# First k of an attention-and-FFN kernel cast and transposed in two parts, the opening in a written order, and batch 0's column blocks partly at full width

## Chip, cores, metric

The kernel runs on one core of one Trainium2 chip. The metric is the device time of one execution in microseconds (us). A profiled execution also has a span, from the first to the last instruction of the program, which is a little shorter than its time.

The engines are named as in the profile: PE is TensorE, which multiplies matrices; PEld is its loading of weights, which runs beside it; DVE is VectorE; ACT is ScalarE; POOL is GpSimd; SP is SyncE. POOL and SP only issue transfers here, but for one small copy of POOL's per batch.

## What is computed

```python
# q, k, v: 8 batches x 12 heads x 448 positions x 64;  w_in: 768 x 2048;  w_out: 2048 x 768
scores = (1 / sqrt(64)) * q @ k.transpose(0, 1, 3, 2)
attn = maximum(scores, 0.0) ** 2 / 448
a = attn @ v                                  # per head 448 x 64
x = a.transpose(0, 2, 1, 3).reshape(3584, 768)
h = x @ w_in
g = 0.5 * h * (1 + erf(h / sqrt(2)))          # exact gelu
out = g @ w_out                               # 3584 x 768, float32
```

There is no softmax: a score goes through a ReLU and a square, so nothing has to be reduced over a row before the product with v.

## The kernel before

**The work of one batch.** The twelve heads make three groups of four (G = 3). For a group, q and k come in with positions on the partitions and are transposed, so that the 64 head dimensions of two heads lie on 128 partitions (qT and kT). A *step* (L523) is one of seven blocks of 64 key positions of a group: four matmuls of 64x64 weights, which stand side by side on PE, against 448 query positions. ACT makes the ReLU with the scale (L535), or DVE does (L537), and DVE squares the result (L544). When all seven steps of a group are squared, 28 matmuls with v (L585) give the group's part of the attention, which DVE (L301) or ACT (L303) copies into xT, already transposed for the FFN. The first FFN matrix works in 16 *column blocks* of 128 (L632): six matmuls over the 768 features each, and a gelu on ACT (L644). The second (L675) works in tiles of 128 tokens over pairs of batches; DVE copies its output, and SP stores it.

**Buffers.** PSUM has three buffers for the attention (tag w: scores and the product with v) and two for everything else (tag f: transposes, column blocks, output tiles). So a set of transposes cannot start until the one before last has been evicted, and a step not until a ReLU has freed its buffer.

**Transposes.** Batches 0 and 1 are transposed by PE with an identity matrix: `add_tk` (L429 in the profile) does the k of a group with 14 small matmuls into one buffer, which one instruction evicts into kT; `add_tq` (L454) does q's. Batches from 2 on are reordered by DVE (pk and pq) and transposed by transfers that SP issues.

**The opening.** The first group's q and k come in float32 over two queues (q32 on SP's, k32 on ACT's), and are cast by `early`: q on ACT, k (896 columns) on DVE. All other loads are issued by POOL and are cast on the way; a program order lists them, and each issue past the eighth waits until the eighth before it has landed. Until data come, PE runs 45 small matmuls on zeros. Batch 0 is worked in two halves of 224 query positions (`halves`): the first half of q for the three groups is loaded and transposed first, and a step of a half is paired with another, so that one ReLU still covers 896 columns. The column blocks of batch 0 are also passed in halves: for each half a pair of blocks (m and m+1) fills one PSUM buffer with 12 matmuls of 224 rows. Batch 1 and later are worked at full width.

**The order.** All work is recorded first as `Op` objects with estimated durations, dependences and the buffers they need. `Scheduler.run` then picks, engine by engine, the operation with the earliest estimated start plus a bias, and at last issues all operations sorted by their estimated start. From batch 2 on the PE order and POOL's order are given as lists (`pe_q`, `pool_q`); for batches 0 and 1 the estimates and biases decide. `order_only` and `later` are conditions for the planner alone: they hold operations back in the plan and put no wait in the program. Engines execute their own instructions in program order.

## Time and profile before

| | |
|---|---|
| median of 6 runs | 393.6 us (392.91 to 394.33) |
| the profiled execution | 392.91 us, of which the span is 391.1 us |
| PE busy | 380.3 us, 97% of the span |
| DVE, ACT busy | 188.3 us (48%), 200.4 us (51%) |
| POOL busy | 45.7 us (12%) |
| granted PE clock | 0.998 of full speed |
| column blocks (L632) | 864 matmuls, 672 with 448 rows and 192 with 224 |
| chain of work that ended last | PE 94%, ACT 2%, DVE 1%, transfers 1% |

The profile page shows an average over the whole span. PE is busy for 97% of it, and what it lacks lies mostly in the first 32 us, so the views that matter are those by stage: busy time of each engine in a window, what an engine waited for, and the instructions in order of time. A matmul's row lasts longer than its place in the pipeline, since its end is modelled; the distance between starts, or the length of a merged run of matmuls, is the better price. The column "idle before" of an instruction tells how long its engine stood still ahead of it and which instruction ended that; "issue" there means that nothing the profile shows was waited for.

### The profile page before, as it was taken

How to read it: one execution, taken by the hardware profiler on the slowest of the kernel's cores; microseconds unless marked ns; L12 is line 12 of the kernel's file. 1: busy time of each engine (PE TensorE's matmuls, PEld its weight loads, DVE VectorE, ACT ScalarE, POOL GpSimd, SP SyncE). 2: the span in 40 equal slices, each digit the busy share in tenths (PEclk: the TensorE clock that was granted, in tenths of full speed). 3: DMA queues.
4: the chain of work that ended last, by engine and by line, in shares of the span. 5: the costliest groups of instructions: out<-in, count | busy, mean ns of one | idle time of the engine just before them, and what ended most of it. 6: DMA issues, size and time to landing. Idle time of an engine off the chain costs nothing.

```text
span 391.1 us, 8085 instructions
## 1 busy us (share of the span) xinstructions
PE 380.3 (97%) x3496; PEld 216.7 (55%) x3497; DVE 188.3 (48%) x348; ACT 200.4 (51%) x304; POOL 45.7 (12%) x69
## 2 busy tenths in 40 slices
PE   6789999999999999999999999999999999999996
PEld 6566784455555555555555555555555555555563
DVE  3989940486636444644555346545355352110121
ACT  3998845754536554565734466366536645222200
POOL 8665304001100200020000200000000000000000
PEclk9999999999999999999999999999999999999999
DMA  9999997999976791689129871370102011100132
GB/s 176 194 203 204 201 195 115 210 200 193 172 136 130 127 178 42 130 145 162 42 65 152 124 136 42 75 148 3 42 21 62 0 42 42 40 15 27 42 80 80
DMA packets 69523, 42.94 MB, mean 110 GB/s; under 512 B 37744, under 2 KB 65904, under 8 KB 69488
## 3 DMA queue, kind: packets, MB, share of 16 engines
q0 software_dynamic: 30512, 22.47, 38.4%
q1 hardware_dynamic: 38672, 19.49, 22.6%
q8 instruction: 27, 0.44, 0.5%
q10 hardware_dynamic: 304, 0.48, 0.3%
q14 instruction: 8, 0.07, 0.0%
HBM read 45.61 MB, written 11.01 MB: 145 GB/s over the span
## 4 chain that ended last, share of the span: by engine, by line
PE 94%; ACT 2%; DVE 1%; DMA 1%; issue 0%
PE psh L632 38%; PE pso L675 38%; PE ps L523 9%; PE pav L585 8%; ACT a_sq L535 2%; DMA k<-in_k_dram 1%; PE tp L429 0%; PE tp L454 0%; DVE xT L301 0%; DVE a_sq L544 0%; DVE a_sq L537 0%; ACT xT L303 0%; ACT qT L303 0%; DVE nk L301 0%; ACT kT L303 0%
## 5 line engine op out<-in xcount | busy, mean ns | idle before, releaser
L632 PE MATMUL psh<-xT,win_sb 128*128 128x448 bf16 (+1 forms) x864 | 154.7, 332 | 0.0
L675 PE MATMUL pso<-wout_sb,h_sb 128*128 128x384 bf16 (+2 forms) x895 | 151.6, 326 | 0.1
L535 ACT ACTIVATE a_sq<-ps 128x896 bf16<-128x896 f32 x142 | 123.9, 916 | 48.2 <-PE ps L523 48.1
L544 DVE TENSOR_TENSOR a_sq<-a_sq 128x896 bf16<-128x896 bf16 (+1 forms) x169 | 100.3, 617 | 53.0 <-ACT a_sq L535 53.0
L644 ACT ACTIVATE h_sb<-psh 128x448 bf16<-128x448 f32 x128 | 70.0, 548 | 99.3 <-PE psh L632 99.0
L675 PEld LDWEIGHTS <-h_sb 128*128 128x128 bf16 x896 | 86.2, 98 | 62.6 <-issue 5.9
L632 PEld LDWEIGHTS <-win_sb 128*128 128x128 bf16 x864 | 81.7, 98 | 65.7 <-issue 9.0
L301 DVE COPY osb<-pso 128x384 f32<-128x384 f32 (+2 forms) x56 | 31.2, 557 | 89.4 <-PE pso L675 89.4
L523 PE MATMUL ps<-qT,kT 64*64 64x448 bf16 (+1 forms) x756 | 47.3, 336 | 3.6 <-ACT a_sq L535 1.3
L537 DVE TENSOR_SCALAR a_sq<-ps 128x896 bf16<-128x896 f32 x27 | 29.4, 1089 | 40.8 <-PE ps L523 40.8
L585 PE MATMUL pav<-a_sq,v_sb 64*64 64x448 bf16 (+1 forms) x756 | 37.1, 330 | 1.6 <-issue 0.9
L523 PEld LDWEIGHTS <-kT 64*64 64x64 bf16 x756 | 18.8, 105 | 24.5 <-issue 17.6
L585 PEld LDWEIGHTS <-v_sb 64*64 64x64 bf16 x756 | 21.2, 107 | 13.9 <-issue 3.8
L301 DVE CAST xT<-pav 128x448 bf16<-128x448 f32 (+1 forms) x29 | 16.0, 558 | 10.6 <-PE pav L585 5.6
L303 ACT CAST xT<-pav 128x448 bf16<-128x448 f32 (+1 forms) x25 | 12.6, 505 | 15.5 <-PE pav L585 9.1
L498 POOL COPY gate<-qT 128x4 bf16<-128x4 bf16 x5 | 0.9, 189 | 158.0 <-DMA qT<-pq 158.0
L250 POOL DMA_DIRECT2D nq<-in_q_dram x14 | 11.6, 830 | 3.5 <-ACT a_sq L535 2.1
L352 POOL DMA_DIRECT2D v_sb<-in_v_dram x14 | 10.6, 759 | 2.4 <-DMA win_sb<-in_moe_w_in_dram 1.7
L334 POOL DMA_DIRECT2D nk<-in_k_dram x13 | 10.0, 769 | 4.7 <-DMA win_sb<-in_moe_w_in_dram 1.1
L390 DVE COPY pq<-nq 112x512 bf16<-112x512 bf16 x36 | 8.2, 283 | 0.0
L379 DVE COPY pk<-nk 128x896 bf16<-128x896 bf16 x18 | 6.2, 384 | 0.0
L775 PE MATMUL spin<-zero 128*128 128x128 bf16 x45 | 4.2, 281 | 1.0 <-DVE zero L762 1.0
(25 smaller groups left out, 42.4 us busy)
## 6 DMA issues: line engine op xcount, KB each, us to landing
nk<-in_k_dram POOLq DMA_DIRECT2D x5, 672.0 KB, 9.1
nq<-in_q_dram POOLq DMA_DIRECT2D x5, 672.0 KB, 11.8
v_sb<-in_v_dram POOLq DMA_DIRECT2D x5, 672.0 KB, 14.2
out_dram<-osb SPq DMA_DIRECT2D x7, 336.0 KB, 2.8
wout_sb<-in_moe_w_out_dram POOLq DMA_DIRECT2D x2, 1152.0 KB, 11.9
out_dram<-osb SPq DMA_DIRECT2D x8, 288.0 KB, 2.9
v_sb<-in_v_dram POOLq DMA_DIRECT2D x9, 224.0 KB, 8.1
out_dram<-osb SPq DMA_DIRECT2D x8, 240.0 KB, 2.8
```

Of the source, the lines that this page charges most:

```text
L250: nc.gpsimd.dma_start(nq[b][:, 4 * g0 : 4 * g1, c0 * D : c1 * D], q_view(b, g0, g1, c0, c1))
L301: V.tensor_copy(dst, src)
L303: A.copy(dst, src)
L352: nc.gpsimd.dma_start(vt[b][:, 2 * g0 : 2 * g1], kv_view(v, b, g0, g1))
L523: nc.tensor.matmul(ps[64 * j : 64 * j + 64, e, x * w : x * w + w], kT[r, g, i * 128 + 64 * j : i * 128 + 64 * j + 64], qT[r, 2 * g + j, co ...
L535: A.activation(ar, ps, AF.Relu, scale=c_att)
L537: V.tensor_scalar(ar, ps, c_att, 0.0, op0=mybir.AluOpType.mult, op1=mybir.AluOpType.max,)
L544: V.tensor_mul(box["a2"][:, :, :used], ar, ar)
L585: nc.tensor.matmul(pav[0][o2 : o2 + 64, e, :w], vt[b][r, 2 * g + e, bass.ts(i, D)], box["a2"][r, e, o : o + w], start=(i == 0), stop=(i == ...
L632: nc.tensor.matmul(ph[:, x * n : x * n + n], win_sb[:, kd, bass.ts(m + x, 128)], xT[b][:, kd, c], start=(kd == 0), stop=(kd == KD - 1),)
L644: A.activation(hT[b // 2][:, m : m + nm, o + c.start : o + c.stop], box[0][:, :S].rearrange("p (x n) -> p x n", x=nm), AF.Gelu,)
L675: nc.tensor.matmul(po[:, :w], hT[pr][:, kf, bass.ts(t, 128)], wout_sb[:, kf, c], start=(kf == 0), stop=(kf == KF - 1),)
```

## The change

There are three parts.

1. The first k is cast in two instructions, 512 columns (blocks 0 to 3) on DVE and 384 (blocks 4 to 6) on ACT, and its transposes are two sets with an eviction each (`K_CUT = 4`). `add_tk` takes a range of blocks, and a step depends only on the set that holds its block.
2. `ORDER` lists all work of the opening, batches 0 and 1 and the loads and reorderings that lie among it. P, A, D, G and S stand for PE, ACT, DVE, POOL and SP; the number is the operation's place in the order in which the kernel records it. The listed operations are issued in the listed order; what is not in the list follows as before. The two planner conditions go. Estimated starting times of engines and landings change too, which are only for the planner.
3. `HALF_M = 6`: only the column blocks 0 to 5 of batch 0 are passed in halves; blocks 6 to 15 are passed one by one with 448 rows, when both halves of batch 0's attention are there.

In the written order, the first operations are: P11, A10 and D12 are the first q's transposes, cast and eviction; D13 and A16 the two casts of k; P14, A15 and P17, D18 the two sets of k's transposes with their evictions; P21 and D22 the q of group 1; P39, P33 and P36 the first steps, with the ReLUs D40, A34 and A37; P19 and P23 are the k transposes of groups 1 and 2. P27, P29 and P31 transpose the second half of q, P129 to P139 batch 1's k and q, and P141 is the first column block.

```diff
-TQ_AFTER = 1
+HALF_M = 6
...
-COLD_END = 4.0
+COLD_END = 0.0
+K_CUT = 4
 SPIN = 45
+ORDER = """
+G0 G1 G2 G3 G4 G5 A10 D13 G6 A16 P11 P14 G7 D12 A15 P17 G8 D18 P21 P39 D22 P33 P36 A34 D40
+P19 D20 A37 P23 G9 P42 P48 D24 P54 A43 D35 A49 P51 D44 P25 D38 A52 D41 G117 A55 D53 P45 D50
+A26 D47 A46 P57 D56 P69 P66 A58 D70 P27 G118 A67 P29 D59 P63 G119 A28 D71 P60 A64 G120 D68
+P78 D61 A62 P75 A79 D65 P81 P31 D30 A76 D80 P96 G121 D32 A97 P72 D77 G122 A82 D98 P129 G123
...
+P205 D230 A209 P261 D182 P251 D183 A262 D210 A206 D233 P202 A252 S237 D207 D232 P226 D234
+A203 D204 S238 S239 P269
+"""
...
-        rest = [o for o in self.open if id(o) not in inside]
+        names = {"P": "PE", "A": "ACT", "D": "DVE", "G": "POOL", "S": "SP"}
+        gone = set()
+        for word in ORDER.split():
+            op, eng = self.open[int(word[1:])], names[word[0]]
+            _, dur, lat = next(e for e in op.engines if e[0] == eng)
+            self.commit(max(self.ready(op), self.free[eng]), op, eng, dur, lat)
+            gone.add(id(op))
+        fixed = {e: [o for o in v if id(o) not in gone] for e, v in fixed.items()}
+        rest = [o for o in self.open if id(o) not in inside | gone]
...
-        for est, op, eng in sorted(self.log, key=lambda x: x[0]):
+        n = len(ORDER.split())
+        for est, op, eng in self.log[:n] + sorted(self.log[n:], key=lambda x: x[0]):
             op.fn(eng)
...
-    def add_tk(b, g, bias=T_BIAS, after=()):
-        box = []
+    def add_tk(b, g, i0=0, i1=NK, bias=T_BIAS):
+        box, n = [], 128 * (i1 - i0)
...
-            for i in range(NK):
+            for i in range(i0, i1):
...
-    ld_k[0, 0] = [early("DVE", lambda: nk[0][:, :2], k32, 4.7)]
-    add_tk(0, 0)
+    ld_k[0, 0] = []
+    for eng, i0, i1 in (("DVE", 0, K_CUT), ("ACT", K_CUT, NK)):
+        c = slice(i0 * D, i1 * D)
+        o = early(eng, lambda c=c: nk[0][:, :2, c], k32[:, :, c], 5.45)
+        ld_k[0, 0] += [o] * (i1 - i0)
+        add_tk(0, 0, i0, i1)
...
-        add_tq(0, g, HC, NC, T_LATE, [later(lambda: AV[0, TQ_AFTER, 0].start)])
+        add_tq(0, g, HC, NC, T_LATE)
...
-        half = [order_only(AV[0, G - 1, 0])]
-        add_tk(1, g, T_ONE, half)
-        add_tq(1, g, bias=T_ONE, after=half)
-    for m in range(0, KF, 2):
+        add_tk(1, g, bias=T_ONE)
+        add_tq(1, g, bias=T_ONE)
+    for m in range(0, HALF_M, 2):
         add_f1(0, m, 0, bias=F1_BIAS)
...
-    for m in range(0, KF, 2):
+    for m in range(0, HALF_M, 2):
         add_f1(0, m, 1, bias=F1B_BIAS)
+    for m in range(HALF_M, KF):
+        add_f1(0, m, bias=F1B_BIAS)
```

## The prediction, made before the result was known

> **What bounds the kernel now.** I read the 40 slices first, then busy time by stage, then what TensorE (PE) waited for, then the opening in order of time. The slices show PE full from the fourth on, while VectorE (DVE) and ScalarE (ACT) are full only in the opening:

> ```profile
> PE   6789999999999999999999999999999999999996
> DVE  3989940486636444644555346545355352110121
> ACT  3998845754536554565734466366536645222200
> ```

> Busy time by stage (length, then PE, PEld, DVE, ACT, POOL with instruction counts, granted clock, DMA share, GB/s):

> ```profile
> 6.00:8.20 2.20, 1.40 (x38) 1.00 (x38) 1.43 (x3) 0.00 (x0) 2.20 (x3) 1.00 1.37 202
> 8.20:12.00 3.80, 2.86 (x88) 2.12 (x84) 3.60 (x6) 3.75 (x5) 3.40 (x6) 1.00 1.43 198
> 12.00:20.00 8.00, 6.31 (x184) 4.74 (x177) 7.42 (x17) 7.77 (x14) 5.23 (x8) 1.00 1.48 192
> 20.00:32.00 12.00, 10.09 (x238) 7.31 (x238) 11.02 (x21) 10.16 (x16) 6.87 (x11) 1.00 1.27 204
> 32.00:58.00 26.00, 25.97 (x354) 20.44 (x349) 20.02 (x39) 19.71 (x31) 7.61 (x11) 1.00 1.28 202
> ```

> From 32 us on PE is the bound (25.97 of 26.00), and the changed order listing is the old one again from batch 1's first column block on; so only PE's idle time before 32 us, and PE work itself, can be won. Idle: 0.80 in 6-8.2, 0.94 in 8.2-12, 1.69 in 12-20, 1.91 in 20-32, together 5.34 us. From 8.2 to 20 us the other two engines hold it: DVE 11.02 and ACT 11.52 of 11.8 us. What PE waited for:

> ```profile
> PE ps L523 <- ACT a_sq L535: 1.3, 3, 0.5
> PE pav L585 <- issue: 0.9, 1, 0.9
> PE ps L523 <- ACT qT L303: 0.7, 2, 0.4
> PE ps L523 <- DVE kT L301: 0.7, 1, 0.7
> PE pav L585 <- ACT a_sq L535: 0.6, 2, 0.3
> ```

> The last number is the longest: no wait is large but the one with no releaser ("issue"). The opening:

> ```profile
> 5.35 0.62 ACT L303 CAST nq<-q 112x512 bf16<-112x512 f32 x1 [2.61 <-DMA q<-in_q_dram]
> 5.52 0.89 DVE L301 CAST nk<-k 128x896 bf16<-128x896 f32 x1 [4.50 <-DMA k<-in_k_dram]
> 6.45 0.39 DVE L301 COPY qT<-tp 128x448 bf16<-128x448 bf16 x1
> 7.09 0.62 DVE L301 COPY kT<-tp 128x896 bf16<-128x896 bf16 x1 [0.24 <-PE tp L429]
> 7.77 0.58 PE L523 MATMUL ps<-qT,kT 64*64 64x224 bf16 x16 [0.72 <-DVE kT L301]
> 8.21 0.92 ACT L535 ACTIVATE a_sq<-ps 128x896 bf16<-128x896 f32 x1 [2.24 <-PE ps L523]
> 8.40 1.09 DVE L537 TENSOR_SCALAR a_sq<-ps 128x896 bf16<-128x896 f32 x1 [0.69 <-PE ps L523]
> ```

> ACT stands still from 5.97 to 8.21 behind a serial chain: cast of k, transposes, eviction of kT.

> **1. Ten column blocks at full width.** Batch 0 issued 16x12 matmuls of 224 rows; now 72 of 224 and 60 of 448: 60 pairs become 60 single ones. Prices, from the chain of waits:

> ```profile
> 51.19 16.09 PE psh L632 x120
> 67.28 0.50 PE ps L523 x8
> 116.11 1.13 PE psh L632 x6
> ```

> Six full ones take 1.13, so 189 ns each. The 120 are 72 halves (six pairs of blocks) and 48 full: (16.09 - 48x0.189)/72 = 97 ns. A pair costs 2x97 - 189 = 5 ns too much; 60 of them 0.3 us (0 if halves are exactly half). The mean durations of the two shapes, 260 and 353 ns, contain the pipeline and would say three times too much per instruction.

> **2. Changes of kind on PE.** Two attention steps (8 matmuls of 448, four side by side, 2x0.19) take 0.50 between column blocks, and the block behind them 1.24 instead of 1.13: about 0.2 us per visit. Counted in the two order listings up to the eighth column block of batch 1, PE changes between transposes, attention and FFN 36 times before and 34 times now: one visit, 0.2 us (0 to 0.3, as places differ).

> **3. First k in two parts.** The listing puts the cast of 512 columns on DVE, 384 on ACT behind the cast of q; then q's transposes, 8 of k's, q's eviction (DVE), the first k eviction (ACT), 6 transposes, their eviction (DVE), the q transposes of group 1, and only then the first step. ACT starts its next instruction about 0.12 before the last one's row ends (five ReLUs of 0.92 in 4.17 us: 0.81 apart), DVE 0.08. The shapes are new. 512 float32 columns on DVE lie between 0.38 (448, bf16) and 0.69 (512 to float32, in the tail): 0.57, so 5.52 to 6.09. 384 on ACT lie between the rows of 224 (0.36) and 448 (0.53): 0.48, so 5.85 to 6.33. The first k eviction (512 on ACT, rows 448: 0.53, 896: 0.91, so 0.58) runs 6.6 to 7.2. The second set needs the buffer that q's eviction frees at 6.84; evicted 7.15 to 7.5. Group 1's q needs the buffer freed at 7.2: 7.25, evicted on DVE 7.6 to 8.0. First step at 7.7 (before 7.77), first ReLU on DVE at 8.0 (8.40), on ACT at 8.1 (8.21). So the split gains little in itself: two waits for buffers replace the long chain. What it gives is work in ACT's empty stretch. By now q of group 1 is evicted as well (0.30 of DVE, formerly at 9.41), and kT of group 1 goes to DVE (0.53) instead of ACT (0.79). DVE is ahead by 0.40+0.30-0.53 = 0.17, ACT by 0.1+0.79 = 0.89. Both bound the stretch, so half the sum: 0.5 us; from 0.1 (the first ReLU alone) to 0.9 (ACT alone).

> [...]

> **4. The "issue" wait.** At 26.05 PE stops inside an AV group for 0.92 us, with no semaphore. The page has 27 packets of 0.44 MB on the instruction queue for 3496+3497 PE instructions: 16 KB, about 259 instructions each. The stall comes 256 instructions after 21.0 us. The three stretches of 256 up to it took 6.6, 5.8 and, without the stall, 4.8 us; with it 6.0. I read it as code that needs about 5.8 to 6.0 us to come while the queues are full. In the changed listing the same 256 hold two pairs of column blocks instead of one; 24 such instructions take 1.26 us, 24 of attention about 0.35. So about 4.8+0.9 = 5.7 us: a stall of 0.3 where 1.1 stood. The stretch ahead loses its only pair, but waits more: near 5.4 us, a stall of up to 0.4 that partly lies under ACT. I take a gain of 0.6; bounds -0.3 (both stall in full) and 1.1 (none).

> [...]

> **5. Order in 20-32 us.** Besides the issue wait, 0.99 us is idle there. Part is its aftermath: ACT idles 0.61 at 27.1 and PE then waits for ACT to free buffers. Another part is ACT's idle 1.13 ahead of a half eviction at 30.98, which waits for DVE's half. In the listing two sets of transposes and three steps follow that AV group, and full-width blocks stand between steps of batch 1. I take 0.4, bounds 0 and 1.0. Behind batch 1's last AV only one block (1.13) instead of six pairs now covers the eviction that batch 1's own blocks need (0.62 on DVE); if it slips, up to 0.6 is lost, and I cost it at nothing.

> POOL and SP carry the same instructions in the same order. Removing the planner's conditions has no instruction of its own.

> **Sum.** 0.3+0.2+0.5+0.6+0.4 = 2.0 us. Span 391.1 to 389.1; the profiled execution 392.91 to 390.9; the median shown, 393.6, lies 0.7 above that execution, so 391.6.

> **Rivals.** (a) *The code packets stay as they are.* One stall of 1 us or two of half remain wherever PE runs attention densely. For it: the cause is the full queues, DMA share 1.2 to 1.5 in every opening stage, and the change moves no load. Against it: the longer stretch. Gain 2.0-0.6-0.4 = 1.0, since the aftermath stays: 392.6. (b) *ACT and DVE bound the opening whatever the order.* For it: 98% and 93% busy from 8.2 to 20 us, and nearly the same work for both. Against it: ACT's 2.2 empty us. Terms 1 and 2 alone: 0.5, so 393.1. (c) *Slower: the order runs into the loads.* Issue plus time to landing gives q's second half at 6.61+8.2 = 14.8, k of batch 1 at 12.58+7.3 = 19.9, its q at 15.40+5.8 = 21.2. Before, PE takes these at 16.38, 21.59 and 24.56, at least 1.6 us later. The new order puts them ahead of other steps, right at their landing, with AV and QK queued behind. Landings later by D cost D once; above 2.0 the kernel is slower, and 3.0 gives 393.6-2.0+3.0 = 394.6. For it: the queue is never empty here. Against it: POOL's issues are the same. That the order is not what it says is excluded by the listing.

> **Chances.** Forecast 0.60, (a) 0.20, (b) 0.13, (c) 0.07. A measurement tells about 0.2% (0.8 us) from no change. Forecast and most of (a) (0.17) count as faster, and 0.02 of (b): 0.79; the rest of (a) and (b), 0.14, as no change; (c) 0.07 as slower. The range runs from a gain of 3.0 (terms 3 to 5 near their upper bounds) to (b)'s 0.5: 390.6 to 393.1.

> **What would show it.** Right: L632 (another line number then) with 804 matmuls; two short casts of k; first step at 7.7, ReLUs at 8.0 and 8.1; the issue wait under 0.5; PE idle in 6-32 us down from 5.3 to about 3.8; first step of batch 2 at 65.3 instead of 67.28. Wrong: PE waiting for nq or nk loads at 15-29 us; a second issue wait; a wait for xT ahead of batch 1's blocks.

## The result, and the profile after

The changed kernel takes 392.5 us in the median of 24 runs (391.77 to 394.38), the kernel before 393.85 us in 54 runs on the same chips (392.62 to 395.45). The ratio is 0.9971, with a 95% interval of 0.9963 to 0.9979: a gain of 1.1 us (0.8 to 1.5), where 2.0 was forecast. The profiled execution took 393.52 us with a span of 391.7; it is one of the longest of its kind, for a reason given below. L632 is now L644 and has 804 matmuls.

The slices of the page, of the changed kernel:

```profile
PE   7899999998999999999999999999999999999996
PEclk9899999999999999999999999999999999999999
```

PE is fuller in the opening, but the tenth slice (88 to 98 us) is an 8 where before all were 9, and the clock has an 8 in the second. Busy time by stage of the changed kernel, with the columns as in the prediction (length, PE, PEld, DVE, ACT, POOL with counts, clock, DMA share, GB/s) and one stage more:

```profile
6.00:8.20 2.20, 1.63 (x42) 1.33 (x46) 0.98 (x3) 1.20 (x3) 2.20 (x3) 1.00 1.34 197
8.20:12.00 3.80, 3.05 (x96) 2.25 (x85) 3.56 (x7) 3.28 (x5) 3.21 (x6) 1.00 1.43 198
12.00:20.00 8.00, 6.49 (x144) 4.63 (x137) 6.94 (x14) 6.82 (x11) 4.99 (x8) 0.79 1.48 192
20.00:32.00 12.00, 11.31 (x276) 8.82 (x273) 11.32 (x23) 10.96 (x18) 7.16 (x11) 1.00 1.26 199
82.00:92.00 10.00, 8.68 (x89) 4.60 (x87) 7.13 (x19) 4.89 (x7) 0.00 (x0) 1.00 1.36 193
```

From 20 to 32 us only 0.69 is idle, where 1.91 was. The clock of 0.79 in the third row is the mean of that stage: it fell to half from 16.0 to 19.4 us. The last row has 1.32 idle between 82 and 92 us, where PE stood still for nothing before:

```profile
82.00:92.00 10.00, 10.00 (x100) 5.50 (x99) 8.21 (x20) 5.75 (x8) 0.00 (x0) 1.00 1.23 196
```

The same stages in a second profile of the changed kernel (e1, span 390.7), with a full clock:

```profile
6.00:8.20 2.20, 1.71 (x46) 1.32 (x50) 1.07 (x3) 1.11 (x3) 2.20 (x3) 1.00 1.36 201
8.20:12.00 3.80, 3.51 (x96) 2.33 (x88) 3.79 (x8) 3.52 (x5) 3.40 (x6) 1.00 1.43 198
12.00:20.00 8.00, 5.72 (x164) 3.97 (x163) 7.50 (x15) 7.48 (x13) 5.15 (x8) 1.00 1.48 193
20.00:32.00 12.00, 11.25 (x257) 8.72 (x251) 11.19 (x22) 10.65 (x18) 6.78 (x11) 1.00 1.27 204
82.00:92.00 10.00, 8.93 (x90) 4.58 (x89) 7.99 (x20) 5.47 (x7) 0.00 (x0) 1.00 1.39 182
```

What PE waited for, changed kernel: the "issue" wait of 0.9 is gone, a wait for DVE's ReLU has come, at 91 us, and one for a load of q, at 15 us.

```profile
PE ps L535 <- DVE a_sq L549: 0.9, 1, 0.9
...
PE tp L465 <- DMA nq<-in_q_dram: 0.5, 1, 0.5
```

The opening of the changed kernel in order of time:

```profile
5.40 0.43 DVE L308 CAST nk<-k 128x512 bf16<-128x512 f32 x1 [4.38 <-DMA k<-in_k_dram]
6.10 0.51 ACT L310 CAST nk<-k 128x384 bf16<-128x384 f32 x1
...
7.93 0.77 PE L535 MATMUL ps<-qT,kT 64*64 64x224 bf16 x24
...
8.37 1.09 DVE L549 TENSOR_SCALAR a_sq<-ps 128x896 bf16<-128x896 f32 x1
8.56 0.92 ACT L547 ACTIVATE a_sq<-ps 128x896 bf16<-128x896 f32 x1 [1.07 <-PE ps L535]
```

The two short casts are there, but the first step is at 7.93 (7.77 before, 7.7 forecast). The first q ended its cast 0.23 later than before, because it landed later; that is not the change.

**Two distances tell the account.** The first matmul of the first output tile (L675, now L687) marks the end of the part that the change moves; from there to the last matmul of the program the work is the same. A distance above 306.56 us is time lost after the opening. The rows of that tile, of before and then of e1:

```profile
80.66 5.37 PE L675 MATMUL pso<-wout_sb,h_sb 128*128 128x384 bf16 x32
```

```profile
78.66 3.59 PE L687 MATMUL pso<-wout_sb,h_sb 128*128 128x384 bf16 x21
```

| profile | first output tile | from there to the last matmul | mean clock |
|---|---|---|---|
| before | 80.66 | 306.56 | full |
| changed | 79.33 | 308.52 | 3.4 us at half |
| changed, second profile (e1) | 78.66 | 308.21 | full |

So the opening gained 2.00 us, the figure of the forecast, and 1.65 of it was given back behind the first output tile. The first output tile itself varies: in the four profiles at full clock that keep this opening or all but its end (e1, e2, e3 and e12) it starts at 78.52 to 78.70, and in the two of before at 80.66 and 80.72, so differences under 0.2 us say nothing. Where the 1.65 went is the first question. The second is why the medians differ by 1.1 to 1.35, when the two profiles at full clock differ by 0.4 in their spans.

**Where it is given back.** In the chain of waits of the changed kernel the load of batch 3's q now stands, 19 us long, ahead of the output tiles:

```profile
67.64 19.33 DMA nq<-in_q_dram
```

The stretch around it in e1, in order of time:

```profile
82.53 0.40 DVE L386 COPY pk<-nk 128x896 bf16<-128x896 bf16 x1 [1.08 <-DMA nk<-in_k_dram]
...
86.01 1.31 DVE L397 COPY pq<-nq 112x512 bf16<-112x512 bf16 x6 [1.48 <-DMA nq<-in_q_dram]
...
89.76 1.09 DVE L549 TENSOR_SCALAR a_sq<-ps 128x896 bf16<-128x896 f32 x1
...
90.90 0.38 PE L535 MATMUL ps<-qT,kT 64*64 64x448 bf16 x4 [0.89 <-DVE a_sq L549]
```

DVE reorders batch 3's k and q (pk, pq), finds them not landed, and stands 1.08 and 1.48 us with output copies, squares and a ReLU queued behind. It never catches up before PE needs that ReLU. Matmul by matmul against before, nearly all of the 1.65 arises between 88.9 and 90.9 us: 0.54 up to the last AV matmuls, which wait for DVE's squares, and 1.09 at the step of the last line above. Before, the same reordering ran without a wait. These rows, first of before and then of e1, follow the lateness back to SP's transposes of batch 2, whose landing releases POOL's gate, behind which batch 3's loads are issued:

```profile
50.52 5.54 SPq L478 DMA_TRANSPOSE kT<-pk  x3
62.81 0.19 POOL L498 COPY gate<-qT 128x4 bf16<-128x4 bf16 x1 [18.67 <-DMA qT<-pq]
84.95 1.29 DVE L390 COPY pq<-nq 112x512 bf16<-112x512 bf16 x6
```

```profile
43.26 11.96 SPq L489 DMA_TRANSPOSE kT<-pk  x3
63.70 0.19 POOL L510 COPY gate<-qT 128x4 bf16<-128x4 bf16 x1 [19.50 <-DMA qT<-pq]
```

The written order starts SP's transposes 7.3 us earlier, and the gate opens 0.89 later (1.86 in the first profile). Batch 3's q lands at 85.98 instead of 84.90, and before it was already used at 84.95: there was no slack.

**Theory A**: that late release, with DVE's order, is the loss. Rivals: DVE is simply overloaded where the first output copies come; or another part of the change, the wide blocks or the split, moves the stage. **Theory C**, formed on the way: the medians also contain a drop of the clock that the change makes rare.

### The profile page after: what moved, and what is told of

It is laid out like the page before. It is cut to its first block, busy times and chain, and to the rows that moved or that the text cites. A ratio compares the mean times of both kernels' runs of the same rounds, so it can differ in the third digit from the quotient of the medians.

```text
span 391.7 us, 7973 instructions
## 1 busy us (share of the span) xinstructions
PE 382.2 (98%) x3436; PEld 212.9 (54%) x3437; DVE 189.5 (48%) x350; ACT 200.2 (51%) x304; POOL 45.7 (12%) x69
## 4 chain that ended last, share of the span: by engine, by line
PE 83%; DMA 8%; DVE 3%; POOL 2%; ACT 1%; SPq 1%; issue 0%; POOLq 0%
PE pso L687 36%; PE psh L644 33%; PE ps L535 7%; DMA nq<-in_q_dram 7%; PE pav L597 7%; DVE a_sq L556 2%; SPq L498 1%; DMA qT<-pq 1%; ACT a_sq L547 1%; POOL nk L341 1%; POOL v_sb L359 1%; DVE a_sq L549 1%; DVE xT L308 0%; POOL nq L257 0%; DVE osb L308 0%
## 5 line engine op out<-in xcount | busy, mean ns | idle before, releaser
L644 PE MATMUL psh<-xT,win_sb 128*128 128x448 bf16 (+1 forms) x804 | 154.3, 344 | 0.1
L687 PE MATMUL pso<-wout_sb,h_sb 128*128 128x384 bf16 (+2 forms) x895 | 151.6, 326 | 0.2 <-DVE osb L308 0.2
L547 ACT ACTIVATE a_sq<-ps 128x896 bf16<-128x896 f32 (+1 forms) x141 | 123.2, 913 | 48.7 <-PE ps L535 48.6
L687 PEld LDWEIGHTS <-h_sb 128*128 128x128 bf16 x896 | 86.3, 98 | 62.6 <-issue 5.9
L644 PEld LDWEIGHTS <-win_sb 128*128 128x128 bf16 x804 | 76.2, 98 | 70.5 <-issue 9.5
L535 PE MATMUL ps<-qT,kT 64*64 64x448 bf16 (+1 forms) x756 | 47.4, 341 | 2.1 <-DVE a_sq L549 0.9
L549 DVE TENSOR_SCALAR a_sq<-ps 128x896 bf16<-128x896 f32 x28 | 30.4, 1089 | 36.0 <-PE ps L535 35.6
L535 PEld LDWEIGHTS <-kT 64*64 64x64 bf16 x756 | 18.7, 107 | 23.7 <-issue 18.7
## 6 DMA issues: line engine op xcount, KB each, us to landing
wout_sb<-in_moe_w_out_dram POOLq DMA_DIRECT2D x2, 1152.0 KB, 11.8
```

The lines of the kernel that those rows point to most:

```text
L535: nc.tensor.matmul(ps[64 * j : 64 * j + 64, e, x * w : x * w + w], kT[r, g, i * 128 + 64 * j : i * 128 + 64 * j + 64], qT[r, 2 * g + j, co ...
L547: A.activation(ar, ps, AF.Relu, scale=c_att)
L549: V.tensor_scalar(ar, ps, c_att, 0.0, op0=mybir.AluOpType.mult, op1=mybir.AluOpType.max,)
L644: nc.tensor.matmul(ph[:, x * n : x * n + n], win_sb[:, kd, bass.ts(m + x, 128)], xT[b][:, kd, c], start=(kd == 0), stop=(kd == KD - 1),)
L687: nc.tensor.matmul(po[:, :w], hT[pr][:, kf, bass.ts(t, 128)], wout_sb[:, kf, c], start=(kf == 0), stop=(kf == KF - 1),)
```

## The experiments

Ratios are to the kernel before on the same chip, with 95% intervals.

**e1, the changed kernel again**, unaltered, for a profile without the drop of the clock.

> The changed kernel once more, unaltered, for a second profile beside the same before. Theory A (the opening gains 2 us or more, and part is lost at 84 to 92 us, where DVE waits in its order for batch 3's k and q): the first output tile (L687) starts at 78.3 to 78.8 us against 80.66 before, the clock stays at 1.00 from 12 to 20 us, and PE idles or stalls 1 to 2.5 us between 84 and 92; ratio 0.996 to 0.998. Theory B (the opening gains only what the time shows, and the waits at 84 to 92 belong to the one profile): first tile at 79.4, no stall over 0.5 us at 84 to 92.

392.59 us, ratio 0.9975 (0.9961 to 0.9989). First output tile 78.66, gate 63.70, given back 1.65: the loss behind the opening is not the clock's.

**e2, batch 3's reordering one half group later**, k and q, and SP's transposes of them with it. A half group is the first four or the last three steps of a group; a batch has six.

```diff
-            n = per * (b - 2) + {2: 2, 3: 2}.get(b, 1)
+            n = per * (b - 2) + {2: 3, 3: 2}.get(b, 1)
```

> Changed kernel, but DVE's reordering of batch 3's k and q stands one half group later in its order, behind the squares and output copies that waited for it; PE's and ACT's orders are the same. Theory A: the waits of DVE for the loads at 82 to 87 us vanish or cost PE nothing, the stall of PE at 84 to 92 falls under 0.5 us, and the time falls by 1 to 2 us against the changed kernel: ratio 0.992 to 0.994. Theory B: same ratio as the changed kernel, 0.997.

391.81 us, ratio 0.9961 (0.9947 to 0.9976). DVE waits for no load any more, and 0.85 is given back instead of 1.65. That rest is one new wait: the reordering now stands in front of two output copies.

```profile
92.95 1.30 PE L687 MATMUL pso<-wout_sb,h_sb 128*128 128x384 bf16 x7 [0.69 <-DVE osb L308]
```

**e3, batch 2's two early key transposes late again**: the two reorderings and transfers go behind each other, as the planner had them.

```diff
-D229 ... S235 ... D231 ... S236 ... P205 D230 ... A252 S237
+P205 D229 D231 D230 ... A252 S235 S236 S237
```

> Changed kernel, but DVE reorders batch 2's first two k groups at about 49 us instead of 43 and 47, so that SP's first two transposing transfers start when most loads have landed. Theory A1 (these early transfers slow the loads, so batch 2's last loads, its last transposes, the copy that releases the next loads and so batch 3's loads all come 2 us later): batch 2's q of the last group lands near 50 instead of 52.9, the release near 62.8 instead of 64.7, batch 3's q near 85 instead of 87, and 0.5 to 1.5 us are won: ratio 0.993 to 0.996. Theory A2 (the release is late because the last q is reordered late in DVE's order, whatever the loads do): release stays at 64 or later, ratio 0.997.

392.1 us, ratio 0.9958 (0.9945 to 0.9971). The gate opens at 62.98, as before; batch 3's q lands at 85.52, still 0.6 later than before, of which the gate explains 0.17; and DVE, with the opening 2 us shorter, is there sooner. Given back: 1.15. So the early transposes cost about 0.5 of the 1.65. What is left, 1.15, fits the shorter opening meeting loads that come no earlier; that part is argued and was not tested by itself.

**e4, all of batch 0's column blocks in halves again**, in the written order: `pairs` maps each of the ten wide blocks to one half of a pair of blocks.

```diff
-        add_f1(0, m, bias=F1B_BIAS)
+        add_f1(0, *pairs[m], bias=F1B_BIAS)
```

> Changed kernel with all sixteen column blocks of batch 0 in halves again: each of the ten full-width blocks in the written order is replaced by a pair of blocks of one half. The prediction's term: 60 pairs at 5 ns, so 0.3 us more than the changed kernel (ratio 0.9979 against 0.9971). Rival: the full blocks matter for the order (a full block takes 1.13 us, a pair 1.26 with its changes of kind), 0.5 to 1 us more: ratio 0.998 to 0.9995. If late loads bound the time (theory A), the loss is hidden and the ratio stays at 0.997.

392.66 us, ratio 0.9983 (0.9968 to 0.9997). First output tile 78.83, 0.17 later than e1 and 0.13 to 0.31 later than the four profiles above: the worth of term 1 lies within its bounds, but is not told from the spread of runs. The loss behind it does not come from the wide blocks; it is larger here (2.07).

**e5, both later**: the edits of e2 and e3 together.

> The changed kernel with both edits: batch 2's two early key transposes behind each other late in the opening, and batch 3's reordering one half group later. Theory A (loads released late, VectorE stands in order in front of them) expects the two gains to overlap, not to add, since both take away the same wait: VectorE waits for no load between 80 and 92 us, TensorE stands under 0.6 us after 82 us, span 389.4 to 389.9, time 391.3 to 391.8. A rival (the stall is VectorE's own load of copies and squares at the first output tiles, the loads only decide where it falls) expects 0.6 to 1.0 us of standing at the output copies again and no gain over the better of the two single edits (391.8).

391.9 us (5 runs), ratio 0.9959 (0.9944 to 0.9973), and 0.84 given back, as in e2. With the loads in time, moving the reordering of keys and queries gains nothing more; the wait at the output copy (0.69) is the price of where the nine copies stand. The two gains overlap, as theory A said, but what is left is what the rival named, DVE's work ahead of the copies.

**e6, the transposes late and only batch 3's queries later**; the reordering of the keys stays. To the edit of e3 comes:

```diff
-            add_pq(b + 1, 0, G, after=at(n))
-            add_T_dma(b + 1, [at(n + (y >= 4)) for y in range(7)])
+            l = n + (b == 2)
+            add_pq(b + 1, 0, G, after=at(l))
+            add_T_dma(b + 1, [at(l + (y >= 4)) for y in range(7)])
```

> The changed kernel with the two early key transposes late, and only batch 3's queries reordered one half group later (its keys as before). Theory A: the query loads land last (85.5 us), so moving their reordering alone takes the second, larger wait (1.45 us of VectorE) away; the wait for keys of 0.6 us stays, and lies under TensorE's work: standing after 82 us under 0.6, time 391.4 to 391.9. Rival: the wait moves to the next in line, 392.1 as with the transposes alone.

391.61 us (4 runs), ratio 0.995 (0.9935 to 0.9965): the lowest median of all, though its interval overlaps those of e2, e3 and e5. In its profiled execution nothing is given back, 306.56 us to a hundredth. But that execution has a clock drop in the opening (0.50 from 20 to 21 us; first tile 79.63), and so comes to the loads about 1 us later than e1. Its other three runs, at clocks of 0.999 and 1.000, have spans of 389.6 to 389.9 us; with a first tile at 78.5 to 78.7 and nothing given back they would be about 389.0 to 389.2 (306.56 and the 3.9 us that every profile has outside the two distances). By this estimate they lose 0.4 to 0.9 again, so that the loss is gone is shown for the longer opening alone. Against e5, whose profile has the same drop (first tile 79.60), the place of the keys' reordering is worth the 0.84. The stage of the profile from 82 us:

```profile
82.00:92.00 10.00, 10.00 (x100) 5.46 (x99) 8.97 (x22) 5.75 (x8) 0.00 (x0) 1.00 1.33 185
```

PE is full while DVE does more in this stage (8.97) than in any other profile of the written order (7.13 to 8.46) or of before (8.21): so DVE's work alone is not the cause; its order and the landings are what differs.

**e7, one cast of the first k**: cast, transposes and eviction of the first k in one part on DVE, the written order otherwise kept. The list loses the second part's operations, and the numbers behind it shift by three.

```diff
-    for eng, i0, i1 in (("DVE", 0, K_CUT), ("ACT", K_CUT, NK)):
+    for eng, i0, i1 in (("DVE", 0, NK),):
```

> The changed kernel, but the first k cast, transposed and evicted in one part on VectorE as before; the rest of the written order unchanged. By term 3 of the prediction (0.5, bounds 0.1 to 0.9) the first ReLUs come later and the first output tile moves from 78.66 to about 79.2, time 392.6 plus 0.3 to 0.5 (the later waits give a part back). Rival: the split is worth nothing in itself, since the first step started no earlier with it (7.93 against 7.77): first output tile within 0.15 of 78.66 and the time within 0.2 of the changed kernel's.

392.97 us, ratio 0.9984 (0.9973 to 0.9994). First output tile 78.66, to a hundredth that of e1; the first step comes even earlier (7.38; q landed 0.31 earlier in this run). In both runs PE waits for the same loads, q's second half at 14.9 (0.30 in e1, 0.22 here) and batch 1's k at 20.68 (0.55 and 0.51): whatever the split wins early is waited for there. By the first output tile the rival is right, and the split is worth nothing that the spread of 0.2 would show. By the time it is the prediction's term: the median is 0.4 above e1's. But that is on another chip with overlapping intervals, and the profiled executions differ by 0.09; whether the split is worth something in the median stays open.

**e8, the wide blocks alone**: the kernel before with only `HALF_M = 6`, the order left to the planner.

> The kernel before with only one part of the change: ten of the sixteen column blocks of batch 0 at full width, the order left to the planner. Term 1 alone: gain of 0.3 us, 393.5 against 393.8, first output tile 80.3 against 80.66. Rival: the planner, which now has wider blocks, loses filler in the opening or lets batch 1 wait for the late blocks: 0.3 to 2 us slower than before.

394.89 us, ratio 1.0041 (1.0025 to 1.0058): slower, the rival's side. First output tile 82.59. PE stops 1.72 us for "issue" at 26 us, has a clock of 0.50 from 28.6 to 32.0, and is idle for 0.89 between 32 and 58 us, where batch 1's steps now wait for evictions and ReLUs. Wide blocks without the order are a loss.

**e9, the kernel before again**, unaltered.

> The kernel before, unaltered, profiled a second time. In 25 of its 44 timed runs so far the mean granted clock is 0.994 to 0.996 and the mean time 394.05 us, in the other 19 it is 0.999 or 1.000 and 393.05; the one profile at hand (392.91) is of the second kind. Theory C: the lower mean is one stretch of 3.4 us at a granted clock of 0.50, which starts where TensorE was used too little over the 3.4 us before it; in this kernel that is the stop for code and what follows (busy 0.53 of the 3.4 us from 25.7), so the stretch should start between 28 and 30 us, and the first output tile come at about 81.6 instead of 80.66, with no stall of TensorE after 82 us in either kind. Rival: the runs differ by something else (loads that land later, the stall at 82 to 92 us that the changed kernel has): then the clock is full in the opening, and TensorE stands after 82 us.

Median 393.62, ratio 0.9998 (0.9984 to 1.0012). The profile fell on a run with a full clock: first output tile 80.72, 306.56 behind it, issue wait 0.82. So it repeats the first profile, and does not show the other kind of run. The timed runs do: of 93 runs of the kernel before in these experiments, 51 have a mean clock of 0.994 to 0.996 and take 394.08 us on average, and 42 have 0.998 to 1.000 and 393.13 us. (The 44 runs of the expectation are 47, 26 and 21 of the two kinds.)

**e10, 40 instead of 45 of the matmuls on zeros** at the start of the kernel before (`SPIN = 40`).

> The kernel before with 40 instead of 45 of the matmuls that only keep TensorE awake at the start: five matmuls and their weight loads fewer ahead of everything. Theory (term 4: TensorE stops every 256 instructions for the next 16 KB of its code, if that has not come): the stop without a releaser keeps its instruction count, not its place in the work, and so moves five matmuls later in the same AV group, after 18 of 28 instead of after 13, at about 26 us and 0.7 to 1.1 us long; time as before, within 0.2%. Rival (the stop belongs to that place, a wait that the profile does not name): it stays after 13 of 28.

393.84 us, ratio 1.0003 (0.9977 to 1.0028). The stop in e9 and in e10:

```profile
25.66 0.54 PE L585 MATMUL pav<-a_sq,v_sb 64*64 64x224 bf16 x13
27.03 0.57 PE L585 MATMUL pav<-a_sq,v_sb 64*64 64x224 bf16 x15 [0.82 <-issue]
```

```profile
25.51 0.67 PE L585 MATMUL pav<-a_sq,v_sb 64*64 64x224 bf16 x18
27.77 0.47 PE L585 MATMUL pav<-a_sq,v_sb 64*64 64x224 bf16 x10 [1.58 <-issue]
```

Five matmuls fewer at the start, and the stop moves from behind the 13th to behind the 18th: it belongs to an instruction count, not to the work. In all five profiles of the planner's order (before, e8 to e11) it stands behind the same number of PE instructions, 957 matmuls and weight loads. Its length, 1.58, was above what was expected. And this execution has the drop that theory C looked for, right behind the stop:

```profile
26.00:29.00 3.00, 0.96 (x28) 1.00 1.34 201
...
30.00:31.00 1.00, 1.00 (x28) 0.50 1.25 206
```

(length, PE, clock, DMA share, GB/s). First output tile 81.98, 1.26 later than in e9: 0.76 by the longer stop; the rest, 0.5, is put down to the matmuls at half clock.

**e11, control**: the edit of e2 on the kernel before.

> Control: the kernel before with the edit that gained 0.8 us on the changed kernel (batch 3's reordering one half group later). In its profile VectorE never waits for batch 3's loads and TensorE does not stand after 82 us, so theory A expects nothing: 393.5 to 394.0, the same as before within 0.2%. If it gains 0.5 us or more here too, the wait for loads is not what the change added.

394.66 us, ratio 1.0022 (1.0009 to 1.0034): not the same but slower, a miss. There is no wait for loads to take away here, and what is left is the edit's own price: of 1.28 lost behind the first output tile, 0.85 is the same wait at the output copy as in e2 (0.69 in the row). The other 0.43 comes at 103.08 us, at a step that waited 0.36 for "issue", and has no cause shown. The edit gains only where the change had put the wait. This run too has a stop of 1.73 and the half clock behind it (0.50 from 30 to 33 us).

**e12, only batch 3's queries later**, the transposes early as in the changed kernel.

> The changed kernel with the one small edit alone: batch 3's queries reordered one half group later, batch 2's early transposes and batch 3's keys as in the changed kernel. Theory A: the loads land as late as in the changed kernel (keys 82.5, queries 86.0), VectorE still waits about 1.1 us for the keys, but no longer for the queries; TensorE's stand of 1.05 us at 89.7 goes, under 0.6 is left after 82 us, first output tile 78.7, time 391.7 to 392.1. If the late release itself is what costs (by way of the transfers of the output weights, say), most of the 1.57 us stays and the time is 392.4 to 392.7.

392.04 us, ratio 0.9959 (0.9947 to 0.997). The time is as expected, the profile is not: the profiled execution (392.68, the longest of six) has the gate at 64.43, queries landing at 86.59, still 1.04 of waiting for them, and 1.93 given back. Half a group later is not late enough when the release is this late. What its shorter runs look like was not seen. Against e6 it suggests that the release and the place of the reordering have to be mended together; e6's later opening differs too.

## Why the prediction was right, and where it was wrong

It was right in sign and range (391.6 forecast, 390.6 to 393.1; 392.5 measured), and the sum of 2.0 for the opening came out at 2.00. That it did so to a hundredth is luck: the parts were not all sized right, and the spread of the marker is 0.2. Nor is the opening the whole kernel. That the median lies within the range owes something to luck too. Of the 1.35 us between the medians about 0.7 is, by an estimate, that runs with a drop of the clock became rare (without them before takes 393.13 on average), and the forecast did not have this. PE's idle time by stage, from the windows:

| us | before | e1 | forecast |
|---|---|---|---|
| 6 to 8.2 and 8.2 to 12 | 1.74 | 0.78 | |
| 12 to 20 | 1.69 | 2.28 | |
| 20 to 32 | 1.91 | 0.75 | |
| sum | 5.34 | 3.81 | 3.8 |
| 82 to 92 | 0.00 | 1.07 | 0 |

- **Terms 1 and 2** (0.3 and 0.2). The opening gained 2.00, of which 1.53 is idle time; 0.47 is left for everything else, work that became shorter among it. Term 1 alone measured 0.17 against e1 (e4; 0.13 to 0.31 against the four profiles), so its 0.3 is neither confirmed nor refuted. Term 2 was not separated.
- **Term 3** (0.5, bounds 0.1 to 0.9), mis-sized and, by e7's profile, with the wrong cause. Up to 20 us the gain is 0.37, but the split has no share in it that the first output tile would show (e7). The cast of 512 columns on DVE took 0.43, not the 0.57 of the sum, yet the ReLUs came at 8.37 and 8.56 (8.29 and 8.48 in e1) instead of 8.0 and 8.1, and of the 0.96 won up to 12 us 0.59 is lost again by 20 us, and more at 20.68, where loads hold PE. "Both bound the stretch" was the false premise: a third bound, the landings, stood close behind ACT and DVE. In e1:

```profile
14.89 0.58 PE L465 MATMUL tp<-ident,nq 112*64 112x112 bf16 x16 [0.30 <-DMA nq<-in_q_dram]
...
20.68 0.58 PE L437 MATMUL tp<-ident,nk 128*64 128x128 bf16 x14 [0.55 <-DMA nk<-in_k_dram]
```

- **Rival (c)'s mechanism is in that loss, at a small price.** PE now waits for q's second half and for batch 1's k, both at their landing, near the times that the rival said (14.8 and 19.9). These waits are also the prediction's first sign of being wrong. They come to 0.85 at most, not 3.
- **Terms 4 and 5** (0.6 and 0.4): 1.16 gained from 20 to 32 us. The "issue" wait is in none of the nine profiles with the written order, and batch 2's first step comes at 65.21 in e1 (65.3 said). So rival (a), whose 392.6 is nearest to the result, is refuted in its mechanism, and term 4's reading as a count of instructions is borne out (e10); that the wait is for code was inferred from the count and is not shown. Term 4 was too small, since all of the stop went, and the stop is not 0.92 in every run. The profiles with the planner's order have 0.82 and 0.92 at full clock, and 1.58, 1.72 and 1.73 where the clock then drops.
- **Costed at nothing and right**: xT's eviction behind batch 1's last AV. PE has no idle time from 32 to 58 us (26.00 of 26.00).
- **Costed at nothing and wrong: the step that failed.** "POOL and SP carry the same instructions in the same order." So they do, but SP's moved in time: 7.3 us earlier, into a queue still full of loads. The step looked at the order of each queue and not at what was in flight beside it, nor at what the gate behind SP's landing releases. Together with an opening 2.0 us shorter, which brings DVE earlier to loads that had come 0.05 us ahead of their use, that gave back 1.65. e2 and e3 took away parts of it, and e6 all in the one execution profiled, whose opening was 1 us longer. How the 1.65 divides between the late landing and the earlier DVE is known only from e3: about 0.5 for the early transposes.
- **The step from profile to median** (0.7) was taken over as a constant. e1's execution misses the forecast for an execution like that of before (390.9) by 1.6, as much as was given back. In the medians only 0.9 is missed, since the 0.7 is no constant: the kind of run with the drop of the clock, 0.95 us longer, is 51 of 93 runs before and 2 of 35 of the changed kernel. How much of the 0.95 is the clock and how much a longer stop ahead of it is not separated (in e10 0.5 and 0.76). That the long stop is the drop's cause in the unaltered kernel is likely from e8, e10 and e11, but no profile of it caught one: this stays open.

## What to carry to other kernels

When an order is rewritten, follow each transfer that starts at another time to what its landing releases, one stage beyond the part that was meant: a shorter opening also brings every later consumer earlier to loads that do not come earlier. Measure the gain at a marker where the changed part ends, and the rest from there, or a loss behind it hides the gain. Where a profile differs from the median by a steady amount, look for what the other runs contain before carrying the difference over.

## What the runs showed of the hardware

**Code.** The stop moved by just the instructions taken away (e10) and took 0.8 to 1.7 us, with the DMA share at 1.3 to 1.4. The page of before has 27 packets with 0.44 MB on the instruction queue, one for 259 of PE's 6993 matmuls and weight loads on average; by the trace PE starts from 159 to 312 of them between one packet and the next. In that profile PE stands with no releaser only once, for 0.92 us. The 256 instructions and 16 KB of e10's theory are the author's estimate from those figures (0.44 MB over 27 packets, 259 instructions each); what the runs show is one stop at a fixed count, 957, and not that PE waits for a packet there.

**Transposing transfers.** Issued at 43.3 and 46.7 us, among loads (e1), two of them took 10.5 and 12.2 us to land; issued at 50.5 and 51.9 (before) they took 6.0 and 5.4. They also held up the loads beside them: the last group of batch 2's q landed at 52.08 in e1 instead of 49.96, and at 50.03 in e3, where the transposes are late again.
